# The in-projection weights of a gMLP block: two casting DMAs on GpSimd's queue in place of eight staged loads and casts

## The chip, the cores and the metric

The kernel runs on one core of one Trainium2 chip. The metric is the device time of one execution in microseconds. A core has five engines with an instruction queue each: TensorE (PE in the profile) for matrix products, VectorE (DVE), ScalarE (ACT) and GpSimd (POOL) for elementwise work, and SyncE (SP), which here only issues transfers. A transfer is issued by an instruction in the queue of SP, ACT or GpSimd and carried out by 16 DMA engines; it adds to a semaphore when its data has landed, and whoever needs the data waits for that.

## What is computed

Block-sparse attention (4 batches, 8 heads, 768 positions, 64 dimensions per head), and a gated MLP on its output:

```
scores = q @ k.T / 8, masked by blocks of 32       # window, first and last block, 3 drawn blocks a row
x      = softmax(scores) @ v, heads side by side   # [4, 768, 512]
h      = relu(x @ w_in)                            # w_in: [512, 1024]
u, v   = h[..., :512], h[..., 512:]
v_n    = (v - mean(v)) / sqrt(var(v) + 1e-6)
v_s    = w_spatial @ v_n + b_spatial               # over the 768 positions
out    = (u * v_s) @ w_out                         # [4, 768, 512]
```

All inputs and the output are fp32 in DRAM. The kernel computes the products in bf16, so every input is cast once.

## The kernel before, in words

**Units of work.** Two heads of a batch make a pair; there are 16 pairs, p = 0 to 15. For each pair, k, q and v are loaded as fp32 into staging tiles (`st_k`, `st_q`, `st_v`, three buffers each; `load`, L104), cast to bf16 by GpSimd (`cast`, L116, the instruction is L135: k and q into `nat`, v into `vv`, six buffers), and k and q are transposed into `kq`, by TensorE and copies of VectorE for pairs 0 to 3, by DMA transposes for the others. For each slice of scores, TensorE multiplies (L405 for the first batch, L418 for the others), ScalarE takes the exponential out of PSUM (L410, L422), TensorE multiplies with v (L451, L469), and VectorE divides by the sum (L433, L434). The result of a pair is transposed into `xt`.

**The gated MLP of a batch** follows its attention. `v_product` and `u_product` multiply `xt` with the two halves of `w_in_t`, four products of 128 rows of w_in each for a block of 128 positions (L543): the v half is columns 512 to 1023 of w_in, the u half columns 0 to 511. The other two products use `w_spt` and `w_out_t`, which are loaded and cast later.

**What sets the order.** The schedule is written by hand. A loop over slots (L795) issues in each slot the scores of this slot, the products with v of an earlier one, what the table `at` lists for it, and a share of the queue of MLP steps (`run_queue`). The first product of batch 0 with `w_in_t` is in slot 15 (`open_first`, the step v0 with rows 0 to 127 of w_in), the next in slots 16, 18 and 20; then the steps of v1, u0 and u1 follow, four each. The loads of pair 4 are in the table at slot 14 and its casts at slot 18; the six pieces of the spatial weights are loaded at slots 16 to 18 (`ws_load`, `ws_f`, six buffers) and cast at slots 19 to 29. Every engine works through its own queue in this order, and an instruction that waits holds up all that is behind it on its engine.

**Ahead of the loop** stand the loads and casts of pairs 0 to 3, and the weights w_in. For these, `w_load` (L220) takes one of six buffers of the tag `osb`, [128, 512] fp32, and issues a load of 256 KB in SP's queue (L222); `w_in_cast` (L227, L228) casts it into `w_in_t`, on GpSimd. The loop at L268 to L274 does this for eight pieces: the v half (u = 0 in the loop) in four row blocks, then the u half. With six buffers, the seventh and eighth load wait for the first two casts. On SP's queue the eight loads stand behind the load of pair 3's v and ahead of the load of `b_col` (L275) and those of pair 4; on GpSimd's queue the eight casts stand behind the casts of pair 2's v, pair 3's v and the rest of pair 0's q (L265 to L267), and ahead of the casts of pair 4. The weights `w_out`, which use the same `w_load`, are loaded at slot 44.

Of the kernel before, what the change touches and what calls it, by code (L numbers as in the profile page):

```python
# [26 lines left out]
def kernel(  # L27
# [16 lines left out]
    nc = tc.nc  # L44
# [8 lines left out]
    DFF = moe_w_in.shape[1]  # L53
    DH = DFF // 2
    NDM = DM // 128
# [21 lines left out]
    w_in_t = const.tile([128, NDM, DFF], BF16)  # L77
# [17 lines left out]
    def dram(src, p, hs=slice(0, 2), cs=slice(0, NCH)):  # L95
        b, g = divmod(p, NG)
        return src[b, 2 * g + hs.start:2 * g + hs.stop].rearrange(
            "h (p c) d -> p h (c d)", c=NCH)[:, :, cs.start * D:cs.stop * D]
# [5 lines left out]
    def load(p, nm, hs=BOTH, cs=ALLC, eng=nc.sync):  # L104
        if (nm, p) not in st:
            st[nm, p] = work.tile([128, 2, S // 2], FP32, tag="st_" + nm, bufs=3, name="st_" + nm)
        eng.dma_start(out=st[nm, p][:, hs, cs.start * D:cs.stop * D],
                      in_=dram(SRC[nm], p, hs, cs))
# [4 lines left out]
    def nat0_view():  # L113
        return nat[0].rearrange("p c h d -> p (c h d)").rearrange("p (h x) -> p h x", h=2)

    def cast(p, nm, eng, hs=BOTH, cs=ALLC):  # L116
        if nm == "v":
            dst = vv[p % NVV][:, hs, cs, 0:D]
        else:
            if p not in nat:  # L120
                nat[p] = work.tile([128, 2 * NCH, 2, D], BF16, tag="nat", bufs=4, name="nat")
            c0 = 0 if nm == "k" else NCH
            dst = nat[p][:, c0 + cs.start:c0 + cs.stop].rearrange("p c h d -> p h c d")[:, hs]
        src = st[nm, p].rearrange("p h (c d) -> p h c d", d=D)[:, hs, cs]
        if p == 0 and nm != "v":
            dst = nat0_view()[:, hs, (c0 + cs.start) * D:(c0 + cs.stop) * D]
            if cs is not C45:
                dst = dst[:, 0].rearrange("p (i t d) -> p t i d", t=2, d=D)
                src = src[:, 0].rearrange("p (t i) d -> p t i d", t=2)
            else:  # L130
                dst = dst.rearrange("p h (c d) -> p h c d", d=D)
        if eng is nc.scalar:
            nc.scalar.activation(out=dst, in_=src, func=AF.Copy)
        else:
            eng.tensor_copy(out=dst, in_=src)  # L135
# [73 lines left out]
    PL, DV = nc.gpsimd, nc.vector  # L209
# [8 lines left out]
    wst = {}  # L218

    def w_load(key, src):  # L220
        wst[key] = work.tile([128, DM], FP32, tag="osb", bufs=6, name="w_f")
        nc.sync.dma_start(out=wst[key], in_=src)  # L222

    def w_in_load(u, g):
        w_load((u, g), moe_w_in[g * 128:(g + 1) * 128, 0 if u else DH:DH if u else DFF])

    def w_in_cast(u, g, eng):  # L227
        eng.tensor_copy(out=w_in_t[:, g, 0 if u else DH:DH if u else DFF], in_=wst.pop((u, g)))  # L228

    def w_out_load(g):  # L230
        w_load(("o", g), moe_w_out[g * 128:(g + 1) * 128, :])
# [30 lines left out]
    load(2, "v")  # L262
    load(0, "q", cs=C45)
    load(3, "v")
    cast(2, "v", PL)  # L265
    cast(3, "v", PL)
    cast(0, "q", PL, cs=C45)  # L267
    pieces = [(u, g) for u in range(2) for g in range(NDM)]  # L268
    for i, x in enumerate(pieces):
        if i >= 6:  # L270
            w_in_cast(*pieces[i - 6], PL)
        w_in_load(*x)
    for x in pieces[2:]:
        w_in_cast(*x, PL)  # L274
    nc.sync.dma_start(out=b_col, in_=moe_b_spatial.rearrange("(p c) -> p c", c=NCH))  # L275


# [486 lines left out]
    def slot_of(p):  # L764
        return S0 + 12 * (p - NG)

    for p in range(NG, NP):
        g = slot_of(p)
# [76 lines left out]
```

## Time and profile before

| | |
|---|---|
| time, median of 3 runs | 215.14 us (213.38 to 216.04) |
| time of the profiled execution | 212.75 us |
| its span, first to last instruction | 210.6 us |
| granted TensorE clock | 0.996 |
| TensorE, matrix products, busy | 201.5 us (96%) |
| ScalarE busy | 169.2 us (80%) |
| VectorE busy | 131.7 us (63%) |
| GpSimd busy | 70.0 us (33%) |
| moved by DMA | 41.82 MB, mean 199 GB/s |

The profile is of one execution. Its page gives for each engine the busy time, the same in 40 equal slices of the span (5.27 us each, in tenths), the chain of work that ended last, the costliest groups of instructions by line, and the transfers. The trace behind it can be asked for the instructions of one engine in order of time: a line of such a timeline has the start, the length, the engine, the line of the kernel, the operation, the tile written and the tile read, the count, and in brackets how long the engine was idle before it and what it waited for. "SPq" is an instruction that issues a transfer. A busy TensorE is not TensorE at its peak, since products are pipelined and their ends are modelled.

### The profile page before, as it was taken

How to read it: one execution, taken by the hardware profiler on the slowest of the kernel's cores; microseconds unless marked ns; L12 is line 12 of the kernel's file. 1: busy time of each engine (PE TensorE's matmuls, PEld its weight loads, DVE VectorE, ACT ScalarE, POOL GpSimd, SP SyncE). 2: the span in 40 equal slices, each digit the busy share in tenths (PEclk: the TensorE clock that was granted, in tenths of full speed). 3: DMA queues.
4: the chain of work that ended last, by engine and by line, in shares of the span. 5: the costliest groups of instructions: out<-in, count | busy, mean ns of one | idle time of the engine just before them, and what ended most of it. 6: DMA issues, size and time to landing. Idle time of an engine off the chain costs nothing.

```text
span 210.6 us, 5243 instructions
## 1 busy us (share of the span) xinstructions
PE 201.5 (96%) x2113; PEld 128.4 (61%) x2146; DVE 131.7 (63%) x291; ACT 169.2 (80%) x224; POOL 70.0 (33%) x104
## 2 busy tenths in 40 slices
PE   8779999999999999999999999999999999999992
PEld 7569878866566665665655655566555655544441
DVE  7899885979454534384986455286785433576541
ACT  4888999999999999979899788979999787266021
POOL 5696669675663304052341040040120000013000
PEclk9999999999999999999999999999999999999998
DMA  5998799999999999999693597696100324610257
GB/s 151 366 367 315 241 337 278 290 221 292 263 376 200 286 197 306 225 300 313 135 229 64 57 315 166 198 294 138 37 3 19 68 53 91 246 53 2 50 132 266
DMA packets 63323, 41.82 MB, mean 199 GB/s; under 512 B 45124, under 2 KB 58052, under 8 KB 63300
## 3 DMA queue, kind: packets, MB, share of 16 engines
q1 hardware_dynamic: 62868, 41.11, 75.2%
q10 hardware_dynamic: 432, 0.39, 0.6%
q8 instruction: 16, 0.26, 0.5%
q14 instruction: 7, 0.06, 0.1%
HBM read 24.38 MB, written 6.29 MB: 146 GB/s over the span
## 4 chain that ended last, share of the span: by engine, by line
PE 89%; DVE 6%; ACT 2%; issue 2%; ACTq 0%
PE ps_moe L543 31%; PE ps L418 22%; PE ps_av L469 12%; PE ps_t L543 8%; PE ps L405 5%; PE ps_sc L543 4%; PE ps_av L451 3%; DVE kq L242 2%; DVE kq L212 2%; PE wps L180 1%; PE ps L291 1%; ACT a_all L410 1%; ACT osb L215 1%; PE ps_av L291 1%; DVE xn L434 0%
## 5 line engine op out<-in xcount | busy, mean ns | idle before, releaser
L422 ACT ACTIVATE a_all<-ps 128x768 bf16<-128x768 f32 x144 | 113.6, 813 | 14.0 <-PE ps L418 7.3
L418 PE MATMUL ps<-kq 88*128 88x384 bf16 x288 | 70.5, 325 | 0.4
L469 PEld LDWEIGHTS <-a_all 128*128 128x128 bf16 x864 | 45.2, 97 | 19.9
L469 PE MATMUL ps_av<-vv,a_all 128*128 128x65 bf16 x864 | 49.8, 193 | 0.0
L418 PEld LDWEIGHTS <-kq 88*128 88x128 bf16 x288 | 28.0, 98 | 31.1 <-issue 0.9
L543 PE MATMUL ps_moe<-w_in_t,xt 128*128 128x512 bf16 x128 | 39.9, 378 | 0.4
L410 ACT ACTIVATE a_all<-ps 128x1024 bf16<-128x1024 f32 x36 | 35.0, 1024 | 2.4 <-PE ps L405 1.8
L543 PE MATMUL ps_moe<-vn,w_spt 128*128 128x512 bf16 x99 | 30.6, 378 | 0.5
L135 POOL CAST nat<-st_k 128x768 bf16<-128x768 f32 (+2 forms) x17 | 14.8, 875 | 44.4 <-DMA st_k<-in_k_dram 44.3
L433 DVE RECIPROCAL rc<-ps_av 128x6 f32<-128x6 f32 (+1 forms) x36 | 6.7, 185 | 28.8 <-PE ps_av L469 27.9
L611 DVE SCALAR_TENSOR_TENSOR un<-ps_moe,b_col,un 128x512 bf16<-128x512 f32 x18 | 13.5, 749 | 16.3 <-PE ps_moe L543 11.7
L405 PE MATMUL ps<-kq 88*128 88x256 bf16 (+1 forms) x140 | 21.6, 275 | 2.1 <-DVE kq L212 1.5
L580 POOL TENSOR_SCALAR std<-mv 128x3 f32<-128x3 f32 (+1 forms) x9 | 2.1, 238 | 60.7 <-DVE mv L577 44.8
L543 PE MATMUL ps_moe<-w_out_t,gt 128*128 128x512 bf16 x66 | 20.2, 378 | 0.2
L543 PEld LDWEIGHTS <-xt 128*128 128x128 bf16 x192 | 15.5, 98 | 7.2 <-DVE xt L212 0.2
L434 DVE TENSOR_TENSOR xn<-ps_av,rc 128x384 bf16<-128x384 f32 (+1 forms) x36 | 18.5, 513 | 1.2
L576 DVE BATCH_NORM_STATS2 stats<-vn 128x6 f32<-128x512 bf16 x24 | 16.5, 687 | 1.4 <-ACT vn L571 0.9
L405 PEld LDWEIGHTS <-kq 88*128 88x128 bf16 x140 | 12.7, 97 | 5.7 <-DVE kq L212 2.0
L135 POOL CAST vv<-st_v 128x768 bf16<-128x768 f32 x16 | 13.5, 844 | 6.9 <-DMA st_v<-in_v_dram 4.2
L135 POOL CAST nat<-st_q 128x768 bf16<-128x768 f32 (+1 forms) x18 | 13.6, 758 | 5.1 <-DMA st_q<-in_q_dram 4.8
L451 PE MATMUL ps_av<-vv,a_all 128*128 128x65 bf16 x288 | 14.5, 193 | 0.4 <-POOL vv L135 0.4
L451 PEld LDWEIGHTS <-a_all 128*128 128x128 bf16 x288 | 13.5, 97 | 2.0 <-issue 0.6
(79 smaller groups left out, 206.1 us busy)
## 6 DMA issues: line engine op xcount, KB each, us to landing
st_v<-in_v_dram SPq DMA_DIRECT2D x16, 384.0 KB, 5.7
out_dram<-osb SPq DMA_DIRECT2D x23, 256.0 KB, 3.0
st_k<-in_k_dram SPq DMA_DIRECT2D x15, 384.0 KB, 4.6
st_q<-in_q_dram SPq DMA_DIRECT2D x15, 384.0 KB, 5.2
ws_f<-in_moe_w_spatial_dram SPq DMA_DIRECT2D x6, 384.0 KB, 7.5
w_f<-in_moe_w_in_dram SPq DMA_DIRECT2D x8, 256.0 KB, 7.1
w_f<-in_moe_w_out_dram SPq DMA_DIRECT2D x4, 256.0 KB, 4.0
st_q<-in_q_dram SPq DMA_DIRECT2D x2, 128.0 KB, 5.1
```

The source lines that it names most:

```text
L135: eng.tensor_copy(out=dst, in_=src)
L405: nc.tensor.matmul(out=ps[:, at:at + n * TW], lhsT=kq[:, h, ci * 128:(ci + 1) * 128], rhs=kq[:, h, qcols(t0, n)], start=True, stop=True)
L410: nc.scalar.activation(out=out, in_=ps, func=AF.Exp, scale=0.125)
L418: nc.tensor.matmul(out=ps[:, hf * 512:hf * 512 + HALF], lhsT=kq[:, j % H, ci * 128:(ci + 1) * 128], rhs=kq[:, j % H, S + hf * HALF:S + (hf ...
L422: nc.scalar.activation(out=a_ref["h", j][:, ci, :].rearrange("p (b c) -> p b c", b=2), in_=ps.rearrange("p (b c) -> p b c", b=2)[:, :, 0:H ...
L433: nc.vector.reciprocal(out=rc[:, 0:n], in_=ps[:, :, D:VA])
L434: nc.vector.tensor_tensor(out=out, in0=ps[:, :, 0:D], in1=rc[:, 0:n].to_broadcast([128, n, D]), op=ALU.mult)
L451: nc.tensor.matmul(out=av_ref[u][:, to, 0:VA], lhsT=a_ref[u][:, at:at + 128], rhs=vv[pp % NVV][:, h, ci, 0:VA], start=(ci == 0), stop=(ci ...
L469: nc.tensor.matmul(out=av_ref[j][:, qc, 0:VA], lhsT=a_ref["h", j][:, ci, qc * 128:(qc + 1) * 128], rhs=vv[p % NVV][:, h, ci, 0:VA], start= ...
L543: nc.tensor.matmul(out=ref["ps"][:, 0:w], lhsT=lhs(i), rhs=rhs(i), start=(i == 0), stop=(i == n - 1))
L576: nc.vector.bn_stats(out=stats, in_=self.vn[:, tcc, :])
L611: nc.vector.scalar_tensor_tensor(out=self.un[:, tcc, :], in0=ps, scalar=b_col[:, tcc:tcc + 1], in1=self.un[:, tcc, :], op0=ALU.add, op1=AL ...
```

## The change

The eight staged loads in SP's queue and the eight casts on GpSimd go. In their place `w_in_load` issues a DMA in GpSimd's own queue that reads the fp32 weights from DRAM and writes them as bf16 into `w_in_t`, with no staging tile. One DMA carries half of w_in: the v half, then the u half, each as [128 partitions, 4 row blocks, 512 columns]. The first stands on GpSimd's queue behind the cast of pair 3's q and ahead of the cast of pair 2's v; the second behind that cast and ahead of the cast of pair 3's v. The first product with `w_in_t` now waits for the whole first DMA, and the first product of u0 for the whole second one. On SP's queue the load of `b_col` follows directly on the load of pair 3's v, and the loads of pair 4 and of the spatial weights follow on that. Nothing is changed on the other engines.

```
-    def w_in_load(u, g):
-        w_load((u, g), moe_w_in[g * 128:(g + 1) * 128, 0 if u else DH:DH if u else DFF])
-
-    def w_in_cast(u, g, eng):
-        eng.tensor_copy(out=w_in_t[:, g, 0 if u else DH:DH if u else DFF], in_=wst.pop((u, g)))
+    def w_in_load(u):
+        cs = slice(0, DH) if u else slice(DH, DFF)
+        nc.gpsimd.dma_start(out=w_in_t[:, :, cs],
+                            in_=moe_w_in.rearrange("(g p) f -> p g f", p=128)[:, :, cs])
...
     load(3, "v")
+    w_in_load(0)
     cast(2, "v", PL)
+    w_in_load(1)
     cast(3, "v", PL)
     cast(0, "q", PL, cs=C45)
-    pieces = [(u, g) for u in range(2) for g in range(NDM)]
-    for i, x in enumerate(pieces):
-        if i >= 6:
-            w_in_cast(*pieces[i - 6], PL)
-        w_in_load(*x)
-    for x in pieces[2:]:
-        w_in_cast(*x, PL)
     nc.sync.dma_start(out=b_col, in_=moe_b_spatial.rearrange("(p c) -> p c", c=NCH))
```

## The prediction, made before the result

> **What bounds the kernel now.** I read the page's engine line and its 40 slices first, then the chain, then the timelines of GpSimd, ScalarE, TensorE and SyncE between 14 and 26 us, where the change lies, and last the stretches of DMA traffic there.
>
> ```profile
> PE 201.5 (96%) x2113; PEld 128.4 (61%) x2146; DVE 131.7 (63%) x291; ACT 169.2 (80%) x224; POOL 70.0 (33%) x104
> ...
> ACT  4888999999999999979899788979999787266021
> POOL 5696669675663304052341040040120000013000
> ...
> PE 89%; DVE 6%; ACT 2%; issue 2%; ACTq 0%
> ```
>
> TensorE holds 89% of the chain. GpSimd, the engine that loses work, is busy a third of the span and is no part of the chain. From slice 4 (16 us) to slice 15 ScalarE is full as well.
>
> ```profile
> 17.41 22.48 ACT L410 ACTIVATE a_all<-ps 128x1024 bf16<-128x1024 f32 x23 [0.28 <-PE ps L405]
> ```
>
> This row of ScalarE's timeline (start, length, what, idle before) has 23 exponentials end to end, 22.48/23 = 0.977 us each, one for each slot of the main loop. So in 17 to 40 us a slot can't be shorter than 0.977 us, and TensorE has hardly any room beside it: whatever makes it wait there is paid to the end.
>
> ```profile
> 14.71 0.82 POOL L135 CAST nat<-st_q 128x768 bf16<-128x768 f32 x1
> 16.93 0.83 POOL L135 CAST vv<-st_v 128x768 bf16<-128x768 f32 x1 [1.40 <-DMA st_v<-in_v_dram]
> 18.39 0.83 POOL L135 CAST vv<-st_v 128x768 bf16<-128x768 f32 x1 [0.63 <-DMA st_v<-in_v_dram]
> 19.16 0.40 POOL L135 CAST nat<-st_q 128x256 bf16<-128x256 f32 x1
> 19.50 4.34 POOL L228 CAST w_in_t<-w_f 128x512 bf16<-128x512 f32 x7
> 24.86 0.61 POOL L228 CAST w_in_t<-w_f 128x512 bf16<-128x512 f32 x1 [1.01 <-DMA w_f<-in_moe_w_in_dram]
> ```
>
> In GpSimd's timeline, what becomes of these rows is the change: the last two go, one DMA comes behind the first and one behind the second.
>
> ```profile
> 18.92 0.41 PE L451 MATMUL ps_av<-vv,a_all 128*128 128x65 bf16 x8
> ...
> 21.76 0.41 PE L451 MATMUL ps_av<-vv,a_all 128*128 128x65 bf16 x8
> 22.00 0.38 PE L543 MATMUL ps_moe<-w_in_t,xt 128*128 128x512 bf16 x1
> 22.22 0.60 PE L405 MATMUL ps<-kq 88*128 88x256 bf16 x4
> ```
>
> These rows of TensorE's timeline are the deadlines: pair 2's v (vv) is read from 18.92, pair 3's from 21.76, and the first product with w_in_t (its v half, row block 0) is at 22.00. No row there waits for GpSimd: the casts were done before. Behind 22.00 in TensorE's queue are the scores (L405) that ScalarE needs for its exponential at 17.41 + 6 x 0.977 = 23.27; they take 0.60, so a late w_in_t is covered for 23.27 - 22.82 = 0.45 us.
>
> **What is removed.** Eight casts on GpSimd, 4.34 + 0.61 = 4.95 us. Nothing on the chain waited for them, and the work behind them on GpSimd (casts of pair 4, spatial weights) waits for loads, so this is worth 0. Eight issues go from SP's queue:
>
> ```profile
> 11.11 10.85 SPq L222 DMA_DIRECT2D w_f<-in_moe_w_in_dram x8
> 22.00 0.43 SPq L275 DMA_DIRECT2D b_col<-in_moe_b_spatial_dram x1
> ```
>
> In this stretch SP waited for staging buffers. Without it the loads of pair 4 and of the six spatial pieces (nine of 384 KB, 3.54 MB) are issued from about 11.5 us instead of 22.48. TensorE and ScalarE show no wait for those loads, so being early gains 0. But it fills the hole in the transfers:
>
> ```profile
> 16.00:20.00 4.00, 3.92 (x75) 3.55 (x72) 3.76 (x11) 3.61 (x4) 2.44 (x4) 1.00 1.02 372
> 20.00:24.00 4.00, 4.00 (x71) 3.56 (x67) 3.03 (x9) 3.96 (x5) 3.71 (x7) 1.00 0.57 161
> ```
>
> The last two figures of a stretch are the DMA engines' busy share and GB/s: full at 372, then 161 where SP was held up. In the changed kernel SP's queue has work of its own (3.54 MB at 366 GB/s, slice 2's rate, are 9.7 us after pair 3's v) while w_in comes on another queue. The bytes read are the same.
>
> **What is added.** Two DMAs on GpSimd's queue, each of 1.05 MB fp32 in 512 rows of 2 KB, which write bf16. No row shows such a DMA, so three costs are bounded.
>
> Issue on GpSimd: SP's plain copy issue takes 0.33 to 0.43 us; the costliest issue in the trace, a DMA transpose on SP, up to 4.05, and its first, at 29.43, 3.28. I take 0.43 and 3.3 as ends and 1.0 as value: it is a plain copy, nearest to SP's row, with four rows per partition instead of one. The first is issued when pair 3's q is cast (14.71 + 0.82 = 15.53). Behind it wait, in order: the v cast of pair 2 (its data landed at 16.93, so up to 1.4 us of issue are hidden), the second DMA, the v cast of pair 3, the q remainder. With 1.0 us they end near 17.8, 18.8, 20.6 (its load delayed by sharing, from 18.39 to about 19.7) and 21.0; the deadlines are 18.92 and 21.76. Cost 0; with 3.3 us the casts end at 19.68 and 23.81 and TensorE waits 0.76 and then 1.29.
>
> Whether VectorE slows the issue:
>
> ```profile
> 8.43 2.88 DVE L242 COPY kq<-kq 24x768 bf16<-24x768 bf16 x4
> ...
> 10.37 1.62 POOL L135 CAST nat<-st_k 128x768 bf16<-128x768 f32 x1
> ```
>
> Beside this SBUF-to-SBUF copy a GpSimd cast took 1.62 instead of 0.82; beside the copies from PSUM (L212, 14.67 to 16.07) the cast at 14.71 took its 0.82. From 15.5 to 18.5 VectorE has only work on PSUM, so I add 0. [...]
>
> Latency: the smallest load,
>
> ```profile
> st_k<-in_k_dram SPq DMA_DIRECT2D x1, 64.0 KB, 2.3
> ```
>
> took 2.3 us from issue to landing, of which 64 KB at 366 GB/s are 0.18; so 2.1 are fixed, including SP's issue of 0.43. With an issue of 1.0 they become 2.7.
>
> Transfer: alone at 366 GB/s 1.05 MB take 2.9 us. SP's queue is full beside it, and at the start, where ACT's and SP's queues ran together, their loads landed alike (2.2 and 2.5 us against 2.3 and 2.6), so neither starved the other. I take half, 183 GB/s: 5.7 us. Ends: 2.9 (whole rate) and 11.5 (a quarter, if the cast or the rows slow it).
>
> **The sum.** First landing 15.5 + 2.7 + 5.7 = 23.9; TensorE waits 1.9 us at the 22.00 product, 0.45 of which ScalarE's lead covers: 1.5 us lost. The second half lands 5.7 later, 29.6; the first product that reads it (u0, the ninth w_in product) was at about 30.96 and is at about 32.5 now: cost 0, with 2.8 us of cover. The profiled execution took 212.75 (its span of 210.6 and 2.15 around it): 214.2 by the sum. The median of the runs is 215.14, so against it **216.6 us**, 0.7% more.
>
> **Rivals.** (1) *Hidden.* The transfer gets nearly the whole rate, or half of it with short latency: landing 15.5 + 2.7 + 2.9 = 21.1, before 22.00; nothing is lost, nothing gained: 215.1. For it: the margin is thin, and SP's loads may be held back by their own waits. Against: 1.02 DMA share with nothing else running. [...]
>
> (2) *Slow cast transfer*, the case clearly slower. The queue of GpSimd gets a quarter of the rate, 91 GB/s, since each 2 KB row is converted on its way or because SP's full queue is preferred: first landing 15.5 + 2.7 + 11.5 = 29.7, loss 7.7 - 0.45 = 7.2; the second half at 41.2 against 30.96 + 7.2, 3.0 more; 10.2 in all: 225.3. It passes 2% (4.3 us) where the first landing is after 26.75, with less than about 123 GB/s, a third of the rate. For it: no row shows a cast on the way, and 3.54 MB of other loads were moved beside it. Against: the two queues at the start were treated alike. An issue of 3.3 us gives 0.76 + 1.29, then a landing at 26.2 against 24.05: 4.2 - 0.45 = 3.8, or 218.9, the upper end of the forecast; longer issues go over to this case.
>
> (3) *Faster.* GpSimd's 5 us and the early loads of pair 4 would have to take a wait from TensorE; the list of waits names none of TensorE's after 16 us, and it is busy for 162.17 of the 164 us from 16 to 180, so 1.8 us, or 213.3, is the most. That the change doesn't do what it says would mean that the casts stay on GpSimd; its list of instructions has none of the eight left.
>
> **How the numbers follow.** Forecast (0.3 to 3.8 us lost, 215.4 to 218.9) 0.43; hidden 0.17; slow 0.36; faster 0.04, which hardly reaches beyond 2%. Within 2% lie forecast, hidden and most of faster, and 2% is about what a measurement of this kernel can tell from no change: its runs spread from 213.38 to 216.04. Slower by over 2%: 0.37; within: 0.60; faster: 0.03. The range starts at 213.4, the lowest of the runs but for hidden or faster, and reaches into the slow case to 223.5, leaving out its far part and a quarter-rate transfer.
>
> **What would show it.** Right: the TensorE product with w_in_t that was at 22.00 waits 1 to 3 us for a DMA, ScalarE shows one gap of that size near 24 us and little else, and the two DMAs take near 1 us each on GpSimd. Hidden: no such wait. Slow: a wait above 4.7 us there, or a second at the ninth w_in product, and a DMA rate of the new queue under 123 GB/s. Issue too long: GpSimd's v casts of pairs 2 and 3 end after 18.92 and 21.76, and TensorE's L451 rows wait for them. What makes me wrong is above all the share of the transfers that the second queue gets.

## The result, and the profile after

| | before | changed |
|---|---|---|
| median of 4 runs each | 214.43 us (213.38 to 216.04) | 223.97 us (222.64 to 225.23) |
| ratio, 95% interval | | 1.0437 (1.0339 to 1.0536) |
| profiled execution, and its span | 212.75, 210.6 | 222.64, 220.8 |
| granted TensorE clock, mean | 0.996 | 0.984 |

The change makes the kernel 4.4% slower. Ratios, here and below, compare mean times and leave out executions that were more than 1.5% above the fastest of their kernel. The forecast was 216.6 us, and its range ended at 223.5. The profiled executions differ by 9.9 us, their spans by 10.2.

The page of the changed kernel, the lines that answer to those of before: engines; the 40 slices, now 5.52 us each, with the granted clock; the chain; and the group of the products with w_in_t:

```profile
PE 206.5 (94%) x2146; PEld 130.3 (59%) x2146; DVE 136.0 (62%) x291; ACT 169.7 (77%) x224; POOL 66.2 (30%) x98
...
ACT  4989159978999999997989888988899878256021
POOL 5797600972368042212416004021201000003000
PEclk9999859999999999999999999999999999999999
...
PE 79%; DMA 12%; DVE 3%; SPq 2%; ACT 1%; POOL 1%; issue 0%; DVEq 0%; ACTq 0%
...
L537 PE MATMUL ps_moe<-w_in_t,xt 128*128 128x512 bf16 x144 | 44.7, 383 | 5.0 <-DMA w_in_t<-in_moe_w_in_dram 4.9
```

Three things are new. ScalarE has a hole in slice 4 (22 us on), the granted clock a dip in slices 4 and 5, and DMA has 12% of the chain, which had none of it before. The group's last column says what these products waited for: 4.9 us for the DMA that loads them.

ScalarE's timeline (start, length, what, idle before), which before was one row of 23 exponentials from 17.41:

```profile
17.21 5.63 ACT L404 ACTIVATE a_all<-ps 128x1024 bf16<-128x1024 f32 x6 [0.28 <-PE ps L399]
28.33 1.02 ACT L404 ACTIVATE a_all<-ps 128x1024 bf16<-128x1024 f32 x1 [5.49 <-PE ps L399]
30.69 1.02 ACT L404 ACTIVATE a_all<-ps 128x1024 bf16<-128x1024 f32 x1 [1.34 <-PE ps L399]
32.26 1.02 ACT L404 ACTIVATE a_all<-ps 128x1024 bf16<-128x1024 f32 x1 [0.54 <-PE ps L399]
33.49 13.91 ACT L404 ACTIVATE a_all<-ps 128x1024 bf16<-128x1024 f32 x14 [0.20 <-PE ps L399]
47.55 1.02 ACT L404 ACTIVATE a_all<-ps 128x1024 bf16<-128x1024 f32 x1
50.05 2.04 ACT L404 ACTIVATE a_all<-ps 128x1024 bf16<-128x1024 f32 x2 [1.47 <-PE ps L399]
```

Since ScalarE paces this stage, its gaps are the bill. The seventh exponential of this stretch is at 28.33; before it was at 17.41 + 6 x 0.977 = 23.27, and the stretch itself began 0.20 earlier here: **5.3 us** go at the first gap. From 28.33 to 33.49 three slots take 5.16 us in place of 2.93: **2.2 us**. The gap at 50.05 is **1.5 us**. The 14 slots between, 33.49 to 47.55, take 14.06 in place of 13.68, 0.4. Behind them the rest of the span is 220.8 - 51.98 = 168.8 here and 210.6 - 42.81 = 167.8 before (51.98 and 42.81 are where the second batch's exponentials start), 1.0 more, which belongs to no one place. Less the 0.2 of the earlier start, the sum is 10.2.

**The first gap.** GpSimd's timeline:

```profile
15.39 0.98 POOL L226 DMA_DIRECT2D w_in_t<-in_moe_w_in_dram  x1
16.86 0.82 POOL L135 CAST vv<-st_v 128x768 bf16<-128x768 f32 x1 [0.48 <-DMA st_v<-in_v_dram]
17.63 0.75 POOL L226 DMA_DIRECT2D w_in_t<-in_moe_w_in_dram  x1
18.38 0.83 POOL L135 CAST vv<-st_v 128x768 bf16<-128x768 f32 x1
```

The issues take 0.98 and 0.75 us, and the two v casts end at 17.7 and 19.2, ahead of their deadlines. What is late is the landing. TensorE's timeline, and the piece of the chain that ends at its wait (start, length, what):

```profile
21.56 0.41 PE L445 MATMUL ps_av<-vv,a_all 128*128 128x65 bf16 x8
26.86 0.59 PE L537 MATMUL ps_moe<-w_in_t,xt 128*128 128x512 bf16 x1 [4.89 <-DMA w_in_t<-in_moe_w_in_dram]
27.24 1.06 PE L399 MATMUL ps<-kq 88*128 88x256 bf16 x4
```

```profile
15.39 11.42 DMA w_in_t<-in_moe_w_in_dram
```

The first DMA lands 11.42 us after its issue. Its first packet moves at 19.61, 4.2 us after the issue, and its last at 26.5. What ran beside it, from the transfers of 15 to 20 us and of 20 to 25 us (queue, packets, MB, share of 16 engines; q0 is GpSimd's new queue, q1 SP's, and a packet of q0 is counted by what it writes: the page has 1056 packets and 1.05 MB for the two DMAs, which read 2.10 MB of fp32):

```profile
q1 hardware_dynamic: 1340, 1.80, 104.8%
q0 software_dynamic: 23, 0.02, 2.8%
```

```profile
q1 hardware_dynamic: 387, 1.04, 59.1%
q0 software_dynamic: 433, 0.44, 52.0%
```

First SP's queue had nearly everything, then the two shared nearly packet by packet. SP's own timeline says why it had so much to move:

```profile
10.87 0.47 SPq L269 DMA_DIRECT2D b_col<-in_moe_b_spatial_dram  x1
11.42 0.40 SPq L107 DMA_DIRECT2D st_k<-in_k_dram  x1
12.55 0.37 SPq L107 DMA_DIRECT2D st_q<-in_q_dram  x1
13.58 0.37 SPq L107 DMA_DIRECT2D st_v<-in_v_dram  x1
14.58 5.16 SPq L503 DMA_DIRECT2D ws_f<-in_moe_w_spatial_dram  x6
```

b_col was issued at 22.00 before. Pair 4's loads are now issued ahead of the first DMA, and the six spatial pieces between 14.58 and 19.74, around its issue at 15.39.

**The dip of the clock.** Stretches (length, then busy time of TensorE's products and weight loads, VectorE, ScalarE, GpSimd with counts, then granted clock, DMA share, GB/s), first of the changed kernel, then of the kernel before:

```profile
22.00:27.00 5.00, 0.14 (x1) 0.11 (x1) 0.60 (x2) 0.84 (x1) 3.35 (x3) 0.90 1.11 307
27.00:33.00 6.00, 6.00 (x49) 4.39 (x48) 2.73 (x8) 2.79 (x3) 0.51 (x1) 0.51 1.36 185
33.00:45.00 12.00, 12.00 (x171) 9.61 (x169) 8.09 (x22) 11.67 (x13) 6.15 (x7) 1.00 0.68 173
```

```profile
27.00:33.00 6.00, 5.95 (x82) 4.72 (x82) 4.96 (x13) 5.91 (x7) 4.09 (x4) 1.00 1.00 349
```

TensorE is busy for all of 27 to 33 us, yet it does 49 products there; before, the same six microseconds had 82 at a clock of 1.00. The four score products at 27.24 take 1.06 in place of 0.60. In steps of 0.02 us the clock reads 0.50 from 26.04, 4.1 us into the wait, to 32.86. So part of the first gap is the clock's too: from the late product to the next exponential it is 28.33 - 26.86 = 1.47 us here, and 27.81 - 26.96 = 0.85 in e8 below, where the clock stayed at 1.00. With these 0.6 the dip costs 2.8 us by the trace.

**The late gap.** GpSimd, then VectorE, then TensorE around 47 us, each from its timeline, and last the same copy and operation of VectorE in the kernel before:

```profile
38.77 0.23 POOL L574 TENSOR_SCALAR std<-mv 128x2 f32<-128x2 f32 x1 [11.26 <-DVE rc L427]
39.08 0.72 POOL L576 TENSOR_TENSOR rstd<-std,mhalf 128x2 f32<-128x2 f32 x1
39.77 3.08 POOL L509 CAST ws_b<-ws_f 128x768 bf16<-128x768 f32 x2
...
45.11 3.44 POOL L509 CAST ws_b<-ws_f 128x768 bf16<-128x768 f32 x2
```

```profile
44.37 0.94 DVE L186 TENSOR_SCALAR vn<-vn,mv,rstd 128x512 bf16<-128x512 bf16 x1
45.23 1.92 DVE L212 COPY kq<-tt 64x1536 bf16<-64x1536 bf16 x1
47.08 1.62 DVE L186 TENSOR_SCALAR vn<-vn,mv,rstd 128x512 bf16<-128x512 bf16 x1
```

```profile
48.95 0.40 PE L445 MATMUL ps_av<-vv,a_all 128*128 128x65 bf16 x8 [1.50 <-DVE xt L212]
```

```profile
37.90 0.54 DVE L212 COPY kq<-tt 64x1536 bf16<-64x1536 bf16 x1
38.36 0.40 DVE L186 TENSOR_SCALAR vn<-vn,mv,rstd 128x512 bf16<-128x512 bf16 x1
```

With all its loads there early, GpSimd waits 11.26 us for the layer norm's statistics and then casts without a pause from 39.77 to 48.55. VectorE's copies from SBUF to SBUF in that time are slow: the copy into kq takes 1.92 where it was 0.54, and the last of the three rows 1.62 where it was 0.40. TensorE waits 1.50 for the copy into xt behind them.

### The profile page after: what moved, and what is told of

Its sections match the earlier page's. It is cut to its first block, busy times and chain, and to the rows that moved or that the text cites. A ratio compares the mean times of both kernels' runs of the same rounds, so it can differ in the third digit from the quotient of the medians.

```text
span 220.8 us, 5259 instructions
## 1 busy us (share of the span) xinstructions
PE 206.5 (94%) x2146; PEld 130.3 (59%) x2146; DVE 136.0 (62%) x291; ACT 169.7 (77%) x224; POOL 66.2 (30%) x98
## 3 DMA queue, kind: packets, MB, share of 16 engines
q0 software_dynamic: 1056, 1.05, 3.5%
## 4 chain that ended last, share of the span: by engine, by line
PE 79%; DMA 12%; DVE 3%; SPq 2%; ACT 1%; POOL 1%; issue 0%; DVEq 0%; ACTq 0%
PE ps_moe L537 31%; PE ps L412 21%; PE ps_av L463 12%; DMA w_in_t<-in_moe_w_in_dram 5%; PE ps_t L537 5%; DMA st_q<-in_q_dram 5%; PE ps L399 4%; PE ps_av L445 3%; PE ps_sc L537 2%; DMA gt<-un 2%; SPq L615 1%; DVE vn L186 1%; DVE kq L212 1%; SPq L107 1%; POOL nat L135 1%; ACT a_all L416 1%
## 5 line engine op out<-in xcount | busy, mean ns | idle before, releaser
L463 PEld LDWEIGHTS <-a_all 128*128 128x128 bf16 x864 | 45.2, 97 | 19.9
L463 PE MATMUL ps_av<-vv,a_all 128*128 128x65 bf16 x864 | 49.8, 193 | 0.0
L537 PE MATMUL ps_moe<-w_in_t,xt 128*128 128x512 bf16 x144 | 44.7, 383 | 5.0 <-DMA w_in_t<-in_moe_w_in_dram 4.9
L412 PEld LDWEIGHTS <-kq 88*128 88x128 bf16 x288 | 28.0, 98 | 31.1 <-issue 0.9
L537 PE MATMUL ps_moe<-vn,w_spt 128*128 128x512 bf16 x108 | 32.7, 378 | 0.0
L135 POOL CAST nat<-st_k 128x768 bf16<-128x768 f32 (+2 forms) x17 | 14.2, 838 | 42.7 <-DMA st_k<-in_k_dram 42.7
L399 PE MATMUL ps<-kq 88*128 88x256 bf16 (+1 forms) x140 | 23.0, 288 | 2.0 <-DVE kq L212 1.6
L427 DVE RECIPROCAL rc<-ps_av 128x6 f32<-128x6 f32 (+1 forms) x36 | 6.6, 184 | 28.0 <-PE ps_av L463 26.8
L537 PE MATMUL ps_moe<-w_out_t,gt 128*128 128x512 bf16 x72 | 21.5, 378 | 0.0
L399 PEld LDWEIGHTS <-kq 88*128 88x128 bf16 x140 | 13.3, 102 | 11.4 <-issue 5.7
L212 DVE COPY kq<-tt 64x1536 bf16<-64x1536 bf16 x24 | 17.5, 729 | 0.3
L445 PE MATMUL ps_av<-vv,a_all 128*128 128x65 bf16 x288 | 15.2, 198 | 1.8 <-DVE xt L212 1.5
L445 PEld LDWEIGHTS <-a_all 128*128 128x128 bf16 x288 | 14.2, 101 | 3.9 <-issue 2.3
```

The costliest lines, as they stand in the source:

```text
L212: nc.vector.tensor_copy(out=o, in_=i)
L399: nc.tensor.matmul(out=ps[:, at:at + n * TW], lhsT=kq[:, h, ci * 128:(ci + 1) * 128], rhs=kq[:, h, qcols(t0, n)], start=True, stop=True)
L412: nc.tensor.matmul(out=ps[:, hf * 512:hf * 512 + HALF], lhsT=kq[:, j % H, ci * 128:(ci + 1) * 128], rhs=kq[:, j % H, S + hf * HALF:S + (hf ...
L445: nc.tensor.matmul(out=av_ref[u][:, to, 0:VA], lhsT=a_ref[u][:, at:at + 128], rhs=vv[pp % NVV][:, h, ci, 0:VA], start=(ci == 0), stop=(ci ...
L463: nc.tensor.matmul(out=av_ref[j][:, qc, 0:VA], lhsT=a_ref["h", j][:, ci, qc * 128:(qc + 1) * 128], rhs=vv[p % NVV][:, h, ci, 0:VA], start= ...
L537: nc.tensor.matmul(out=ref["ps"][:, 0:w], lhsT=lhs(i), rhs=rhs(i), start=(i == 0), stop=(i == n - 1))
```

## The experiments

Three theories for the landing after 11.4 us were told apart. Q: the loads that SP has queued ahead and beside. F: a fixed start of some 4 us of a DMA from GpSimd's queue. C: a transfer that casts is slow by itself. Two further terms, the clock and the late gap, were tried by themselves. All edits are against the changed kernel, and ratios are to the kernel before, run on the same chip.

### e1_sp_held: SP's later loads wait for the first DMA

A copy of a few columns of w_in_t goes into SP's queue ahead of b_col, so that b_col and all behind it are issued when the first DMA has landed.

```
+    hold = const.tile([128, 8], BF16, name="hold")
+    nc.sync.dma_start(out=hold, in_=w_in_t[:, 0, DH:DH + 8])
     nc.sync.dma_start(out=b_col, in_=moe_b_spatial.rearrange("(p c) -> p c", c=NCH))
```

> The changed kernel with SP's queue held, behind the load of pair 3's v, until the first casting DMA has landed (a 16-byte copy on SP that reads w_in_t); the 3.5 MB of later loads then don't run beside it. In the changed kernel the first DMA was issued at 15.39 us, its first packet moved at about 19.6 and it landed at 26.8. Theory Q (the loads that SP has queued take its turn and then half of the rate): the first packet comes by 18.4, when the last load ahead is through, the transfer alone takes about 3.2 us, it lands near 22, TensorE waits below 0.7 us for it, and the kernel takes 214 to 216 us. Theory F (a DMA of GpSimd's queue starts some 4.2 us after its issue, whatever else runs): first packet at 19.6, landing near 23.4, a wait of 1.5 us, no fall of the clock, 215.5 to 217.5 us. Rival C (the cast itself is slow): landing after 26, and 222 us or more.

Measured: 214.24 us, ratio 0.9992 (0.9943 to 1.0041). Of the whole 4.4% nothing is left. The casting DMA is as before, issued at 15.76, but its first packet moves 1.7 us later instead of 4.2, and it lands at 21.3. The transfers of 15 to 20 us, then the answer on the tile w_in_t (shortest, median, longest; the changed kernel had 11.4 and 16.0 at the ends), then TensorE's and ScalarE's rows:

```profile
q0 software_dynamic: 367, 0.38, 57.7%
q1 hardware_dynamic: 339, 0.39, 23.5%
```

```profile
DMA to landing us min/median/max: 5.5/6.3/7.0
```

```profile
22.18 0.38 PE L539 MATMUL ps_moe<-w_in_t,xt 128*128 128x512 bf16 x1
```

```profile
17.59 25.56 ACT L406 ACTIVATE a_all<-ps 128x1024 bf16<-128x1024 f32 x26 [0.28 <-PE ps L401]
```

The product with w_in_t waits for nothing, and 26 exponentials stand end to end, over the place of the late gap too: GpSimd's spatial casts are spread out again. The clock is 1.00 throughout. Q holds; F and C fall as the main cause, since neither the queue nor the cast was changed. This also clears VectorE, which has the same copies beside the issue in both kernels.

### e8_first_uncast: the first DMA without its cast

The v half is moved as fp32 into a staging tile, and GpSimd casts it in four steps; the tag osb has four buffers to make room.

```
-    w_in_load(0)
+    wf = work.tile([128, NDM, DH], FP32, tag="wf", bufs=1, name="wf")
+    nc.gpsimd.dma_start(out=wf, in_=moe_w_in.rearrange("(g p) f -> p g f", p=128)[:, :, DH:DFF])
...
     cast(0, "q", PL, cs=C45)
+    for g in range(NDM):
+        nc.gpsimd.tensor_copy(out=w_in_t[:, g, DH:DFF], in_=wf[:, g])
```

> The first DMA of GpSimd's queue writes fp32 into a staging tile of its size, so nothing is cast on the way, and four casts on GpSimd follow; the output staging has four buffers instead of six for the room. If the cast on the way makes the DMA slow, the plain DMA lands more than 1.5 us sooner after its issue than the 11.4 us of the changed kernel. If the queue and what runs beside it make it slow, it lands 10.5 to 12.5 us after its issue all the same, and the kernel is slower than the changed one by the first cast, 0.6 us or a little more: 223 to 227 us.

Measured: landed 10.1 us after the issue, first packet after 3.8; 219.35 us in its single execution. Both are below what was expected for a slow queue, and the landing is 1.3 us sooner than 11.4, short of the 1.5 that stood for a slow cast. The start is nearly as late without a cast, so the cast doesn't explain it. What the cast adds to the transfer is less sure: in the profiles of e2, e6, e7, r2, r3 and r4 below, which keep the casting DMA and SP's loads, it landed 12.2 to 12.6 us after its issue. So between 1.3 and 2.5 us can be the cast's. TensorE:

```profile
26.96 0.38 PE L540 MATMUL ps_moe<-w_in_t,xt 128*128 128x512 bf16 x1 [3.28 <-POOL w_in_t L271]
```

Behind this wait of 3.28 us the granted clock stayed at 1.00, and the product takes its 0.38 where it took 0.59 in the changed kernel. That is why it was faster than expected, together with a late start of that execution, told below.

### e5_held_behind_pair4: pair 4's loads ahead, the spatial weights held

The copy of e1 is moved to slot 15, behind the loads of pair 4.

```
+    hold = const.tile([128, 8], BF16, name="hold")
+    when(15, lambda: nc.sync.dma_start(out=hold, in_=w_in_t[:, 0, DH:DH + 8]))
```

> SP's queue held until the first casting DMA has landed, as in e1_sp_held, but behind the three loads of pair 4: at the issue of the casting DMA the same loads lie ahead of it as in the changed kernel, and the six spatial loads (2.4 MB) no longer run beside it. Theory: two things make the landing late, the loads ahead (first packet 4.2 us after the issue in the changed kernel, 1.7 in e1_sp_held) and the loads beside (half of the rate). Here the first packet still comes about 4 us after the issue; what is left of pair 4 by then (0.8 MB) and the 1.05 MB take 5 us, so it lands near 24.8, TensorE waits 2.5 to 3 us, the clock stays full, and the kernel takes 216.5 to 219. If only the spatial loads beside it counted, 214 to 215.5; if only the loads ahead, 222 to 224.

Measured: 216.67 us, ratio 1.014 (1.0075 to 1.0205), as expected, between e1 and the changed kernel. First packet after 2.7 us (4 was expected), landing 7.7 after the issue. By this one execution the loads that lie ahead at the issue are not all that delays the start: with the spatial loads held the start took 2.7 us, and 4.2 in the changed kernel, where SP adds them behind it. The loss grew with what SP had queued: the ratio was 0.9992 with all held (e1), 1.014 here and 1.0437 in the changed kernel. Its profiled execution was 1.7 us late from the start and so shows no wait at the product; the cause of the 1.4% rests on the times alone.

### e3_v_staged: the first half as it was

The v half goes back to four loads of SP and four casts of GpSimd; the u half stays a casting DMA.

```
-    w_in_load(0)
     cast(2, "v", PL)
     w_in_load(1)
     cast(3, "v", PL)
     cast(0, "q", PL, cs=C45)
+    for g in range(NDM):
+        w_half_load(g)
+    for g in range(NDM):
+        w_half_cast(g)
```

> The v half of w_in staged as before (four fp32 loads on SP behind pair 3's v, four casts on GpSimd), the u half by the second casting DMA at its place. Theory: all of the loss comes from the late landing of the first half. The v half is there before 22 us, the u half lands before 31, no product with w_in_t waits, and the time is that of the kernel before within 0.5% (213.5 to 215.5). Rival: a casting DMA costs by itself, through its issue on GpSimd or by the transfers beside it: 1% or more above the kernel before.

Measured: 214.5 us, ratio 1.0011 (0.9959 to 1.0064). No cost of the second DMA shows, and the interval leaves it 0.6%, 1.4 us, at most: nearly all of the loss hangs on the first. Here four loads of SP stand ahead of the early ones, so this agrees with Q but doesn't tell it from C. The one profiled execution, of 220.18 us, has the late gap all the same, on ScalarE:

```profile
46.35 2.03 ACT L413 ACTIVATE a_all<-ps 128x1024 bf16<-128x1024 f32 x2 [1.48 <-PE ps L408]
```

VectorE's three rows take 0.95, 1.92 and 1.62 there. If the other executions have this gap too, it is not worth its full 1.5 us at the end; no trace of one of them was kept.

### e4_first_at_head: the first DMA ahead of everything

```
+    nc.gpsimd.dma_start(out=w_in_t[:, :, DH:DFF],
+                        in_=moe_w_in.rearrange("(g p) f -> p g f", p=128)[:, :, DH:DFF])
...
-    w_in_load(0)
```

> The changed kernel with the first casting DMA at the head of GpSimd's queue, ahead of the first iota, where no transfer is queued yet. Theory Q: it starts moving within 2.5 us of its issue. Theory F: its first packet comes about 4.2 us after its issue here too. Either way it has landed long before 22 us and no product with w_in_t waits for it; 1.05 MB are now moved beside the first loads, which are on the way to the first exponential, at up to 2.9 us. Time 214.5 to 217.5, against 224 with the DMA at its place.

Measured: 218.25 us, ratio 1.0193 (1.0098 to 1.0288), a little above the range expected; it is slower than the kernel before, but whether by 2% the interval leaves open. The wait at w_in_t is gone: issued at 1.23, first packet 2.4 later, landed at 8.3. Two costs are left, as its list of waits, ScalarE's timeline and the chain at its start show:

```profile
PE ps_av L447 <- DVE xt L215: 1.5, 1, 1.5
```

```profile
19.54 6.54 ACT L406 ACTIVATE a_all<-ps 128x1024 bf16<-128x1024 f32 x7 [0.28 <-PE ps L401]
```

```profile
1.23 0.98 POOL w_in_t L137
...
2.35 0.16 POOL eq L170
```

The eleventh exponential of the kernel is at 19.54 instead of 17.41, 2.1 us later, and the first is so already, at 8.02 instead of 5.88. The chain up to there has no load in it: it runs through the issue of this DMA and the mask work behind it on GpSimd's queue, whose first instruction starts at 2.35 instead of 0.83, and through score products that take 1.04 us instead of 0.60. So it is the place in GpSimd's queue, and not first of all the sharing of the DMA engines, that costs these 2.1 us. The late gap is still there with its 1.5. Sum 3.6, and the medians differ by 218.25 - 214.64 = 3.6; but the profiled spans differ by 215.7 - 210.6 = 5.1, so that the two agree so well is partly chance. The late gap does not come from the DMA wait, which is gone here. It comes with SP's early loads: with all of them held (e1) or the spatial ones (e5), the list of TensorE's waits doesn't have it.

### e2_warm and e6_casts_moved: the clock, and the late gap

e2 puts 80 products of zeros, whose result nobody uses, ahead of the first product with w_in_t, so that TensorE isn't idle while it would wait:

```
         filler(80, psum.tile([128, 512], FP32, tag=moe_tag(), bufs=1, name="wps"))
```

> The changed kernel with 80 small matrix products of zeros (128x128, some 4.5 us at the full clock) ahead of the first product with w_in_t, so that TensorE works while it would wait. Their output is used by nobody. Theory: of the 10 us that the change costs, about 2.2 are the half clock that was granted from 26.9 to 32.7 us after the wait of 4.9 us; here the clock stays full, the exponentials follow each other at 0.98 us from the landing on, and the kernel takes about 2 us less than the changed one, 221.5 to 222.5, ratio to the kernel before 1.033. Rival: ScalarE hides the half clock, or the later stall is what counts: less than 0.7 us gained.

Measured: 221.32 us, ratio 1.032 (1.0236 to 1.0403), about as expected. The clock is 1.00 in all of 22 to 36 us.

e6 takes four of the six casts of spatial pieces off the time of VectorE's copies: two go to an earlier slot, two to a later one, and the transposes that read them follow.

```
-    for i, (ld, ca) in enumerate([(16, 19), (16, 21), (17, 23), (17, 25), (18, 27), (18, 29)]):
+    for i, (ld, ca) in enumerate([(16, 19), (16, 21), (17, 21), (17, 21), (18, 38), (18, 39)]):
...
-    for i, sl in enumerate((23, 27, 31)):
+    for i, sl in enumerate((23, 27, 40)):
```

> The changed kernel with four casts of spatial weights moved on GpSimd's queue: the third and fourth ahead of the first rstd, behind which they waited 11 us in the changed kernel, the fifth and sixth behind the second rstd of the next blocks. In the changed kernel GpSimd casts without a pause from 39.8 to 48.5 us, beside it three SBUF-to-SBUF operations of VectorE (44.4 to 48.7) take 4.5 us instead of some 1.4, and TensorE waits 1.5 us for VectorE. Theory: with GpSimd free in that stretch they take their usual time, the wait of 1.5 us goes, and the kernel takes 1.5 us less than the changed one, ratio to the kernel before 1.033 to 1.04. Rival: the wait is hidden by what comes later, no change, 1.044.

Measured: 222.85 us, ratio 1.0433 (1.0381 to 1.0485), more than expected. VectorE:

```profile
46.33 0.40 DVE L186 TENSOR_SCALAR vn<-vn,mv,rstd 128x512 bf16<-128x512 bf16 x1
46.65 0.55 DVE L212 COPY kq<-tt 64x1536 bf16<-64x1536 bf16 x1
47.11 0.40 DVE L186 TENSOR_SCALAR vn<-vn,mv,rstd 128x512 bf16<-128x512 bf16 x1
```

Without GpSimd's casts beside them the same three take 0.40, 0.55 and 0.40 in place of 0.94, 1.92 and 1.62, and TensorE's 1.50 for xt is gone. In this execution, though, the wait for the DMA was 6.0. The mechanism is shown, its worth in time isn't.

### e7_warm_casts_moved, and all four on one chip

e7 has both edits.

> Both edits together: the 80 small products ahead of the first product with w_in_t and the moved casts. Theory: the parts add up. The half clock (2.6 us by e2_warm) and the second wait (1.5) go, the wait for the DMA (4.9 to 5.5) stays: 219.5 to 220.5 us, ratio to the kernel before 1.024 to 1.028. Rival: the parts hide each other, and it is no better than e2_warm at 1.032.

Measured: 220.05 us, in the range expected, at a ratio of 1.0312 (1.0259 to 1.0364), above it. Since the changed kernel, e2, e6 and e7 had not all been timed together, four more runs set them side by side, in five rounds on one chip: the changed kernel, e2's edit, e6's edit, and both.

> The changed kernel once more, on one chip with the three others of this call, so that the parts of its loss can be compared directly. 222.5 to 224.5 us, ratio to the kernel before 1.04 to 1.047.

> e2_warm once more beside the changed kernel. Theory: 2.2 to 2.6 us below it for the half clock. Rival: less than 0.7.

> e6_casts_moved once more beside the changed kernel; against the kernel before its ratio was 1.0433, that of the changed one 1.0437, from different calls. Theory: the wait for VectorE near 47 us costs 1.5 us, so 1.2 to 1.8 us below the changed kernel. Rival: what it costs is hidden later, within 0.5 us of it.

> Both edits once more beside the changed kernel. Theory: the gains of r2 and r3 add up, 3.4 to 4.4 us below the changed kernel, and what remains above the kernel before is the wait for the DMA, 5 to 6 us. Rival: no better than r2.

| | us | ratio to before (214.29) | interval |
|---|---|---|---|
| r1_changed | 224.46 | 1.0487 | 1.0437 to 1.0536 |
| r2_warm | 221.08 | 1.0361 | 1.0309 to 1.0413 |
| r3_casts_moved | 222.30 | 1.0429 | 1.0372 to 1.0486 |
| r4_warm_casts_moved | 220.36 | 1.0317 | 1.0273 to 1.0360 |

The changed kernel itself comes out above its expected ratio of 1.04 to 1.047. Keeping TensorE busy is worth 1.0487 - 1.0361 = 1.26%, 2.7 us (the medians differ by 3.4), and the intervals don't meet: the clock's part is shown. It agrees with the 2.8 us of the trace. One caution: the mean clock of r1's executions is 0.967 to 0.981, below the 0.984 of the profile above, so they seem to have a second dip like those of the last section. Without it the difference stays: the changed kernel's executions at a mean clock of 0.983 to 0.984 took 222.64 to 224.48 us, those of e2 and r2 at 0.998 to 1.00 took 220.09 to 221.08. Moving the casts is worth 0.58%, 1.2 us, with intervals that overlap: likely, by the trace, but not shown by the times. Both together give 1.70%, 3.6 us, about the sum. What is left, 3.17% or 6.8 us, has no other named part than the wait for the first DMA, 5.3 in the changed kernel's profile and 5.4 in r4's (the exponential due at 17.55 + 6 x 0.977 = 23.41 is at 28.76). The 1.5 us between are within what single executions differ by (in e6 the DMA landed 12.6 us after its issue, not 11.4, and TensorE waited 6.0), and are not assigned.

## Why the prediction was wrong

**Right.** The issue on GpSimd: 1.0 forecast, 0.98 and 0.75 measured. The casts behind it: no wait, as forecast. The work removed was worth nothing: e1, which has it removed too, runs at 0.9992 of the kernel before. The share: half was taken, and 433 packets stand against 387 in 20 to 25 us. The second half: it lands at 33.6 and isn't waited for. The place too was right: TensorE at the product due at 22.00, paid by ScalarE, and ScalarE's lead of 0.45 did cover that much (5.3 us of gap less 0.6 for the clock are 4.6, for a product 5.1 late against a start 0.2 earlier).

**Latency, the step that failed first.** "With an issue of 1.0 they become 2.7" was taken from the smallest load of SP, at the head of the program, where nothing was queued. The first packet alone took 4.2 here, and the transfer 26.5 - 19.6 = 6.9 in place of 5.7; landing 11.4 after the issue in place of 2.7 + 5.7 = 8.4. Of the 3.0 us more, 1.8 are the latency's and 1.2 the transfer's, and 1.9 of waiting became 4.9. With SP held the latency is right: 2.7 and the 2.9 of the whole rate make 5.6, and e1 measured 5.5. e1 and e5 show that the start isn't a constant: 1.7 us with SP held, 2.7 with pair 4 queued, 4.2 with everything queued. The prediction had the fact in hand (3.54 MB in SP's queue beside it) and used it for the rate, not for the start. It also read the row of SP's eight loads as a wait for staging buffers; SP's list of waits gives GpSimd's casts, which free the buffers, 2.0 us of it, and the landing of earlier loads 5.6.

**A term that was missing: the clock.** A wait was priced at its own length. TensorE's wait of 4.9 us also cost 2.8 us by the trace, 2.2 of them in the three slots behind the first gap, and 2.7 by r1 and r2. In the runs here a wait of 3.28 us (e8) left the clock at 1.00, one of 3.6 (r3_casts_moved) brought it down to 0.56 in 28 to 30 us, and one of 4.9 to 0.50. No run shows a fixed time for the fall or for the return. The fall came 3.3 us into the wait in r3 and 4.1 in the changed kernel. In e6 it came sooner: its wait of 6.0 began at 22.7 and the clock read 0.67 in 24 to 26, so about 2 us into the wait, an estimate that takes 1.00 before the fall and 0.50 behind it. The return took 3.0 us of work in r3 (28.63 to 31.65) and 6.0 in the changed kernel (26.86 to 32.86).

**"So being early gains 0."** Early loads were priced as a gain only. They cost twice: they are what delayed w_in, and they let GpSimd's casts run together beside VectorE's SBUF copies, a gap of 1.5 us at 50 us whose worth in the whole time the runs don't show. The prediction had one direction of this in hand (beside such a copy a GpSimd cast took 1.62 in place of 0.82), but asked it only of GpSimd, and only around the issue. The other direction is what the changed kernel shows: VectorE's copy into kq took 1.92 us beside GpSimd's casts, and 0.55 without them in e6.

**The rivals.** *Hidden* is wrong for this kernel, but it is what e1 gives, at 214.24. *Slow cast transfer* had a time, 225.3, close to the 223.97, and its point of decision, a first landing after 26.75, was just passed at 26.8. But its mechanism, a quarter of the rate from casting or from SP's preference, and a second wait at u0, isn't what happened: while it moved, the transfer had half the engines (52.0% in 20 to 25 us), and u0 waited for nothing. SP's full queue went first only ahead of the start: 1340 of its packets beside 23 in 15 to 20 us. The time was near by luck: a transfer too slow and a second wait that didn't come made up for the missing clock and late gap.

## What to carry to other kernels

The staged loads also held back what was behind them on SP's queue, while they waited for buffers (2.0 us before the change) and for loads ahead of them to land (5.6 us): b_col was issued at 22.00, and at 10.87 without them. Before taking such loads out, ask which transfers will now run early, and keep them behind the urgent one, by order in one queue as before the change, or by a wait as in e1. Price a new wait of TensorE that is longer than e8's 3.28 us, which left the clock at 1.00, with a slower clock behind it as well (0.50 behind the 4.9 us of the changed kernel), and take the latency of a transfer from a row with the same load on the other queues (the first packet came after 1.7 us in e1, after 4.2 in the changed kernel).

## What was not expected of the hardware

The start of the first DMA from GpSimd's queue differed with what SP's queue held: 1.7 us after the issue with it held (e1), 2.4 at the empty head of the program (e4), 2.7 with three loads queued (e5), 3.8 (e8) and 4.2 (the changed kernel) with all nine. In the changed kernel it moved 23 packets beside SP's 1340 in 15 to 20 us, then from 20 us 433 beside 387. Why the even sharing begins only then is open; no run here tells it. What SP holds is not all of the start either: in e1 only 20 packets had moved by 18.25, and the bulk followed from there, 2.5 us after the issue, with only 16 packets of SP's in the microsecond before.

TensorE's clock was also halved near the start of some executions, with work to do: in the profiled ones of e2, e5, e8, r2 and r3 it read 0.50 in 12 to 14 us, and the kernel's eleventh exponential (17.21 in the changed kernel) was 1.7 to 3.2 us later. The kernels differ nowhere before that in what TensorE is given to do. What differs is how densely it worked: in 8 to 12 us it was busy for 1.8 to 2.1 us in e5, e8, r2 and r3, whose clock fell between 11 and 12, and for 2.7 to 2.9 us in the changed kernel, e1, e6, e7 and r4, whose clock stayed at 1.00; in e2 it did nothing from 9 to 10 and the clock fell between 10 and 11. That the sparse work is the cause is likely by this, but was not tried. Such a late execution waits less for w_in, since its deadline has moved too, and this makes single executions of these kernels poor evidence for differences under 3 us.
